# First MLP layer of the last two token groups by a seven-product scheme, with the former score banks as working space

## The chip, the cores and the metric

The kernel runs on one core of a Trainium2 chip. The core has a matrix engine (TensorE, here PE), a vector engine (VectorE, DVE), an engine for functions (ScalarE, ACT), GpSimd (POOL) and a queue engine (SyncE, SP). Matmul results land in PSUM, eight banks of 128 partitions x 512 f32; everything else lies in SBUF. The metric is the device time of one execution in microseconds, as the median of several runs.

## The reference

Attention with causal mask and 16 extra "beacon" keys, then a two-layer MLP with a sigmoid gelu on all 4608 tokens:

```
scores = (1/8) * q @ concat(beacon_k, k).T      # 8 batches, 8 heads, 576 queries, 592 keys, 64 wide
a      = softmax(masked scores)
x      = (a @ concat(beacon_v, v))  -> (4608, 512)
h      = x @ w_in                               # 512 -> 2048
g      = h * sigmoid(1.702 * h)
out    = g @ w_out                              # 2048 -> 512, float32
```

## The kernel before, in words

**Attention.** A set is four heads of one batch; there are 16 sets. `e_qk` (L437) writes a chunk of scores of a set into the tile `s`, which is four PSUM banks as one tile of 128 x 4 x 512 (L438); `e_exp` (L455) has ACT read all four banks and write the exponentials to SBUF (`E`, three buffers). POOL masks (L479), DVE adds up columns (L497), PE multiplies with the values (`e_av`, L528, matmul L534), DVE divides (L546 to L569) and writes the result, transposed, into `xT`, a ring of 2304 tokens.

**MLP.** Tokens go in groups, `GROUPS` (L576): two of 256 and then eight of 512; groups 8 and 9 are the last. The first layer of a group of 512 (`e_m1`, L582) has 16 tiles of 128 rows of `h`, each in a PSUM bank of its own and made of four matmuls of 512 columns (L593). ACT reads the bank and writes gelu to `g` (`e_gelu`, L611). The second layer of groups 2 to 9 is done already by a Strassen-Winograd scheme of seven products of halves (`products`, L947): DVE makes sums of quarters of `g` (`e_s`, L681, L658) and once of `w_out` (`e_t`, L665); `e_prod` (L693) does a product in four blocks of four matmuls of 256 columns (L707); `e_half` (ACT, L715) and `e_join` (DVE, L720) gather the products from PSUM, and `e_store4` (L728) has SP store a quarter of the group's output.

**PSUM.** Four banks are the score tile `s` (pool `pss`). The other four, `u0` to `u3` (pool `psu`), are a ring of `RING` = 4: every tile of `e_av`, `e_m1` and `e_prod` takes one of them (`ring_tile`, L349), which comes free when its last reader ("closer") is done.

**Order.** The kernel first describes all operations as `Op`s with engine, duration and dependencies. The order of each engine's queue is written out by hand in `ORDER` (L16), by numbers of operations. `Plan.run` (L147) goes through these lists with assumed durations; it settles which ring bank a tile takes and the order in which the instructions are emitted. The tile framework then puts in the semaphore waits, from what each instruction reads and writes of which tile, in the order of emission. The hardware runs every queue in its order, with these waits.

The lines that set bank and order:

```
def ring_tile(key):
    if key not in rings:
        i = plan.tiles[key]
        rings[key] = psu.tile([P, 512], F32, tag=f"u{i}", name=f"u{i}")
    return rings[key]
```

Of the kernel before, what the change touches and what calls it, by code (L numbers as in the profile page):

```python
# [10 lines left out]
ALU = mybir.AluOpType  # L11
# [7 lines left out]
        170, 173, 176, 145, 125, 148, 150, 177, 182, 188, 191, 227, 194, 197, 232, 183, 203, 234, 200, 178, 237,  # L19
        179, 206, 258, 241, 209, 184, 263, 185, 212, 265, 213, 248, 246, 268, 214, 215, 401, 251, 253, 272, 218,  # L20
        404, 275, 244, 279, 219, 220, 407, 282, 284, 277, 221, 414, 320, 296, 304, 290, 302, 292, 300, 298, 312,
        308, 294, 318, 314, 310, 306, 316, 426, 435, 423, 343, 338, 339, 340, 433, 431, 438, 344, 345, 359, 349,
        341, 464, 346, 350, 351, 352, 354, 574, 355, 429, 360, 361, 577, 356, 362, 357, 372, 365, 583, 474, 477,
        373, 366, 374, 367, 605, 480, 484, 375, 482, 607, 368, 506, 502, 488, 492, 610, 490, 486, 498, 504, 500,
        508, 514, 510, 516, 494, 496, 512, 534, 593, 596, 535, 536, 539, 540, 550, 541, 542, 537, 742, 545, 546,
        547, 548, 603, 745, 551, 552, 553, 599, 601, 619, 622, 748, 555, 556, 557, 558, 561, 755, 625, 627, 629,
        562, 563, 776, 568, 564, 569, 570, 571, 779, 764, 767, 659, 637, 641, 657, 649, 651, 647, 661, 635, 631,
        653, 805, 772, 770, 774, 643, 655, 633, 639, 645, 679, 680, 815, 818, 700, 681, 682, 684, 701, 915, 690,
        685, 686, 691, 692, 702, 918, 687, 693, 695, 703, 696, 924, 821, 823, 697, 698, 706, 946, 825, 707, 713,
        708, 709, 948, 934, 937, 714, 715, 716, 827, 951, 944, 940, 942, 853, 831, 833, 855, 857, 851, 843, 835,  # L30
        837, 847, 839, 845, 829, 849, 841, 1083, 960, 963, 875, 876, 880, 877, 878, 881, 882, 1086, 968, 966, 970,
        883, 1089, 902, 909, 903, 886, 891, 1096, 887, 888, 889, 892, 893, 1117, 904, 894, 905, 896, 897, 1120, 898,
        899, 910, 911, 1105, 1108, 1146, 912, 976, 994, 996, 972, 978, 1000, 992, 982, 974, 998, 990, 984, 988, 980,
        1002, 986, 1256, 1156, 1113, 1111, 1115, 1159, 1025, 1020, 1026, 1021, 1259, 1022, 1027, 1031, 1023, 1028,
        1265, 1164, 1162, 1166, 1041, 1042, 1287, 1036, 1047, 1032, 1048, 1033, 1037, 1038, 1034, 1039, 1289, 1054,
        1055, 1049, 1056, 1043, 1044, 1050, 1292, 1057, 1198, 1172, 1168, 1178, 1184, 1180, 1194, 1170, 1174, 1176,
        1275, 1278, 1182, 1186, 1196, 1188, 1190, 1281, 1301, 1285, 1283, 1304, 1216, 1217, 1221, 1192, 1222, 1227,
        1218, 1223, 1228, 1219, 1224, 1232, 1229, 1233, 1230, 1307, 1311, 1309, 1237, 1327, 1333, 1238, 1243, 1234,
        1244, 1235, 1323, 1239, 1245, 1250, 1251, 1341, 1240, 1246, 1252, 1253, 1337, 1405, 1315, 1331, 1343, 1411,
        1335, 1321, 1403, 1431, 1313, 1325, 1407, 1419, 1317, 1423, 1425, 1319, 1339, 1421, 1409, 1329, 1361, 1413,  # L40
        1366, 1382, 1429, 1362, 1363, 1401, 1367, 1364, 1427, 1368, 1383, 1372, 1369, 1373, 1374, 1375, 1388, 1377,
        1389, 1378, 1390, 1395, 1379, 1384, 1380, 1385, 1391, 1396, 1415, 1397, 1398, 1470, 1454, 1417, 1455, 1449,
        1471, 1450, 1451, 1476, 1452, 1456, 1477, 1457, 1478, 1460, 1461, 1462, 1463, 1465, 1466, 1467, 1468, 1472,
        1479, 1473, 1483, 1484, 1485, 1486,
# [3 lines left out]
        195, 198, 233, 235, 201, 204, 238, 180, 207, 259, 210, 264, 186, 266, 269, 216, 402, 405, 408, 222, 417,  # L48
        415, 297, 291, 303, 305, 301, 299, 293, 309, 321, 295, 319, 313, 315, 311, 307, 317, 436, 439, 342, 465,
        468, 575, 578, 584, 587, 606, 608, 503, 507, 489, 491, 493, 487, 499, 505, 509, 515, 517, 495, 501, 511,  # L50
        497, 513, 611, 538, 743, 746, 749, 756, 758, 777, 780, 660, 642, 638, 652, 658, 648, 650, 636, 632, 662,
        654, 806, 644, 634, 656, 640, 646, 809, 916, 683, 919, 928, 925, 947, 949, 952, 828, 832, 854, 856, 852,
        858, 834, 838, 844, 840, 836, 846, 830, 848, 850, 842, 1084, 879, 1087, 1090, 1099, 1097, 1118, 1121, 1147,
        1150, 977, 995, 979, 997, 993, 973, 975, 983, 991, 999, 989, 1001, 981, 1003, 985, 987, 1257, 1260, 1024,
        1269, 1266, 1288, 1290, 1293, 1199, 1179, 1173, 1181, 1185, 1195, 1171, 1169, 1175, 1177, 1183, 1187, 1197,
        1189, 1191, 1193, 1220, 1328, 1334, 1324, 1342, 1316, 1332, 1344, 1406, 1412, 1338, 1336, 1404, 1432, 1314,
        1408, 1420, 1318, 1424, 1326, 1426, 1320, 1340, 1422, 1410, 1330, 1322, 1414, 1430, 1402, 1365, 1428, 1416,
        1418, 1453,
# [3 lines left out]
        123, 163, 160, 124, 224, 169, 128, 166, 172, 175, 146, 147, 126, 149, 151, 225, 226, 398, 190, 193, 196,  # L62
        199, 255, 256, 257, 202, 205, 286, 242, 411, 287, 211, 208, 243, 399, 249, 247, 400, 250, 412, 254, 252,
        273, 245, 274, 280, 276, 413, 281, 285, 283, 278, 289, 461, 288, 462, 419, 580, 420, 463, 326, 327, 328,
        421, 322, 92, 323, 324, 422, 427, 428, 424, 425, 325, 330, 334, 329, 335, 432, 336, 331, 434, 337, 332, 333,
        470, 347, 582, 353, 471, 581, 472, 430, 473, 358, 363, 475, 476, 478, 479, 481, 485, 739, 483, 369, 376,
        370, 589, 752, 740, 590, 615, 518, 753, 921, 519, 754, 526, 591, 527, 520, 528, 592, 529, 521, 741, 522,
        597, 523, 594, 530, 595, 598, 531, 802, 532, 524, 533, 616, 543, 525, 604, 549, 617, 618, 554, 600, 620,
        602, 623, 624, 621, 559, 760, 628, 761, 762, 626, 630, 565, 763, 566, 768, 572, 765, 811, 812, 766, 803,
        804, 769, 773, 771, 671, 1080, 775, 672, 813, 922, 663, 814, 664, 675, 667, 816, 673, 819, 668, 669, 817,  # L70
        923, 665, 666, 820, 674, 676, 677, 1093, 670, 688, 694, 678, 930, 822, 824, 699, 931, 826, 932, 933, 704,
        710, 938, 939, 935, 936, 717, 711, 945, 941, 943, 1081, 956, 957, 958, 871, 1082, 1094, 1095, 959, 872, 873,
        867, 859, 961, 962, 964, 965, 860, 863, 1262, 1143, 861, 874, 862, 868, 864, 967, 865, 971, 866, 969, 884,
        869, 870, 1101, 1144, 890, 1145, 1102, 895, 1103, 1104, 900, 906, 1109, 907, 1110, 913, 1106, 1107, 1152,
        1153, 1004, 1154, 1005, 1155, 1264, 1006, 1263, 1016, 1012, 1017, 1157, 1114, 1112, 1013, 1018, 1116, 1160,
        1008, 1161, 1009, 1019, 1158, 1014, 1015, 1029, 1010, 1165, 1011, 1007, 1163, 1167, 1035, 1040, 1271, 1051,
        1045, 1058, 1052, 1297, 1272, 1273, 1274, 1298, 1299, 1276, 1279, 1300, 1200, 1204, 1280, 1201, 1277, 1205,
        1282, 1302, 1206, 1286, 1284, 1208, 1305, 1209, 1202, 1303, 1210, 1212, 1203, 1306, 1207, 1213, 1225, 1231,
        1308, 1312, 1214, 1310, 1215, 1211, 1236, 1247, 1241, 1248, 1254, 1349, 1345, 1350, 1346, 1347, 1353, 1351,
        1354, 1355, 1356, 1357, 1358, 1359, 1370, 1348, 1360, 1352, 1376, 1381, 1386, 1392, 1393, 1445, 1446, 1433,  # L80
        1399, 1437, 1434, 1438, 1447, 1435, 1441, 1442, 1436, 1443, 1444, 1439, 1448, 1440, 1458, 1464, 1469, 1480,
        1474, 1481, 1487,
    ],
    "POOL": [
        8, 10, 12, 14, 16, 17, 19, 21, 23, 25, 27, 29, 31, 33, 35, 37, 39, 41, 43, 45, 47, 110, 49, 51, 113, 114,
        53, 55, 57, 59, 133, 61, 136, 137, 63, 65, 67, 69, 71, 378, 230, 231, 229, 380, 382, 384, 386, 236, 388,
        390, 392, 239, 240, 394, 396, 261, 260, 262, 441, 443, 270, 267, 271, 449, 451, 453, 455, 457, 459, 403,
# [29 lines left out]
class Plan:  # L117
# [6 lines left out]
    def __init__(self, ring):  # L124
        self.ops = []
        self.ring = ring
        self.tiles = {}
        self.closers = {}
# [76 lines left out]
def kernel(  # L205
# [27 lines left out]
    HF = S // 2  # L233
    NKT = DMODEL // P
    NNT = DFF // P
    RING = 4

    NE, NB2, NB3 = 3, 2, 3

# [893 lines left out]
```

## Time and profile before

| what | value |
|---|---|
| median of 3 runs | 329.16 us (329.14 to 329.3) |
| span of the profiled execution, first to last instruction | 327.2 us |
| median less span (the profile shows no other time of its own execution) | 1.96 us |
| instructions | 9966 |
| granted TensorE clock, mean of the span | 0.999 |
| last score chunk's exponentials | before 250 us |
| last matmul, last join, end | 323.4, 324.1, 327.2 us |

Times inside the run count from the span's start. A line such as `L707 PE MATMUL u<-w,g ... x160 | 21.7, 273 | 0.0` is a group of instructions: source line, engine, operation, tiles written and read, shape, count; then busy us and mean ns of one; then the idle time of the engine in front of them and who ended it. PE's matmuls overlap in a pipeline, so a duration (273 ns) is longer than the step from one to the next. In the chain of waits every piece of time from the end of the run backwards is put down to the instruction that held up the next one.

### The profile page before, as it was taken

How to read it: one execution, taken by the hardware profiler on the slowest of the kernel's cores; microseconds unless marked ns; L12 is line 12 of the kernel's file. 1: busy time of each engine (PE TensorE's matmuls, PEld its weight loads, DVE VectorE, ACT ScalarE, POOL GpSimd, SP SyncE). 2: the span in 40 equal slices, each digit the busy share in tenths (PEclk: the TensorE clock that was granted, in tenths of full speed). 3: DMA queues.
4: the chain of work that ended last, by engine and by line, in shares of the span. 5: the costliest groups of instructions: out<-in, count | busy, mean ns of one | idle time of the engine just before them, and what ended most of it. 6: DMA issues, size and time to landing. Idle time of an engine off the chain costs nothing.

```text
span 327.2 us, 9966 instructions
## 1 busy us (share of the span) xinstructions
PE 314.6 (96%) x4364; PEld 214.7 (66%) x4364; DVE 237.2 (72%) x480; ACT 202.1 (62%) x236; POOL 113.9 (35%) x178
## 2 busy tenths in 40 slices
PE   6589999999999999999999999999999999999995
PEld 6467665545775477746878878547764776447884
DVE  4838798777987989977998798858558853006674
ACT  1676697678767586679666786868577212674010
POOL 8765478190419312941177019400042000000000
PEclk9999999999999999999999999999999999999999
DMA  7999999293424911792039709500120012000122
GB/s 126 159 201 211 204 186 184 37 123 107 99 72 64 190 34 34 79 198 43 7 53 178 119 4 124 154 2 3 34 98 0 2 34 83 15 0 2 65 98 97
DMA packets 58220, 28.83 MB, mean 88 GB/s; under 512 B 41280, under 2 KB 53568, under 8 KB 58176
## 3 DMA queue, kind: packets, MB, share of 16 engines
q0 software_dynamic: 47552, 18.49, 47.9%
q1 hardware_dynamic: 10560, 9.69, 9.2%
q8 instruction: 34, 0.56, 0.7%
q14 instruction: 10, 0.08, 0.1%
q10 hardware_dynamic: 64, 0.01, 0.0%
HBM read 37.22 MB, written 9.44 MB: 143 GB/s over the span
## 4 chain that ended last, share of the span: by engine, by line
PE 83%; DMA 6%; DVE 4%; POOL 3%; ACT 2%; issue 1%; ACTq 0%; POOLq 0%
PE u L593 34%; PE u L707 30%; PE u L534 9%; PE s L447 7%; PE u L638 3%; DMA w<-in_moe_w_out_dram 3%; DMA w<-in_moe_w_in_dram 3%; ACT E L458 1%; DVE sA L658 1%; DVE g L626 1%; POOL vb L378 1%; POOL w L384 0%; DVE bkn L403 0%; ACT L614 0%; DVE kT L418 0%
## 5 line engine op out<-in xcount | busy, mean ns | idle before, releaser
L593 PE MATMUL u<-xT,w 128*128 128x512 f16 (+1 forms) x704 | 130.6, 341 | 0.6 <-ACT g L614 0.5
L458 ACT ACTIVATE E<-s 128x2048 f16<-128x2048 f32 (+5 forms) x66 | 98.9, 1515 | 44.9 <-PE s L447 44.4
L614 ACT ACTIVATE g<-u 128x512 f16<-128x512 f32 x128 | 70.5, 598 | 53.7 <-PE u L593 53.2
L593 PEld LDWEIGHTS <-w 128*128 128x128 f16 x704 | 67.6, 98 | 54.3 <-issue 1.9
L479 POOL TENSOR_SCALAR_AFFINE_SELECT E<-E 128x512 f16<-128x512 f16 (+3 forms) x78 | 49.3, 665 | 110.8 <-ACT E L458 79.1
L723 DVE SCALAR_TENSOR_TENSOR osb<-u,osb 128x512 f32<-128x512 f32 x56 | 37.3, 683 | 24.5 <-PE u L707 22.5
L707 PEld LDWEIGHTS <-g 128*128 128x128 f16 x512 | 48.3, 98 | 9.3 <-issue 0.2
L707 PE MATMUL u<-w,g 128*128 128x256 f16 x384 | 50.6, 273 | 0.0
L447 PE MATMUL s<-qT,kT 32*128 32x32 f16 (+20 forms) x1376 | 34.6, 228 | 5.7 <-ACT E L458 2.8
L447 PEld LDWEIGHTS <-kT 32*128 32x128 f16 x1376 | 25.2, 92 | 22.5 <-issue 14.4
L707 PEld LDWEIGHTS <-sA 128*128 128x128 f16 x384 | 36.3, 98 | 5.3 <-issue 0.3
L707 PE MATMUL u<-tB,sA 128*128 128x256 f16 x256 | 35.1, 273 | 0.1
L658 DVE TENSOR_TENSOR sA<-g 128x512 f16<-128x512 f16 x32 | 12.9, 416 | 26.2 <-ACT g L614 26.2
L569 DVE TENSOR_TENSOR xT<-u,rz 128x352 f16<-128x352 f32 (+2 forms) x52 | 25.5, 517 | 6.5 <-PE u L534 6.3
L378 POOL DMA_DIRECT2D vb<-in_v_dram x32 | 27.4, 876 | 2.4 <-DMA qn<-in_q_dram 1.6
L534 PE MATMUL u<-E,vb 128*32 128x352 f16 (+8 forms) x928 | 27.4, 262 | 0.0
L497 DVE TENSOR_TENSOR zs<-zs,E 128x1344 f16<-128x1344 f16 (+2 forms) x36 | 22.7, 633 | 5.3 <-POOL E L479 4.4
L534 PEld LDWEIGHTS <-vb 128*32 128x32 f16 (+1 forms) x928 | 19.9, 96 | 5.5 <-issue 1.7
L418 DVE STREAM_TRANSPOSE kT<-kn 128x576 f32<-128x576 f32 x16 | 20.1, 1257 | 2.1 <-DMA kn<-in_k_dram 1.4
L418 DVE STREAM_TRANSPOSE qT<-qn 128x576 f32<-128x576 f32 x16 | 19.9, 1241 | 0.3 <-DMA qn<-in_q_dram 0.3
L546 DVE STREAM_TRANSPOSE zt<-u 128x224 f32<-128x224 f32 (+2 forms) x32 | 15.0, 470 | 5.9 <-PE u L534 5.8
L497 DVE TENSOR_TENSOR zs<-E 128x1856 f16<-128x1856 f16 x12 | 15.8, 1320 | 3.3 <-POOL E L479 3.3
(48 smaller groups left out, 252.3 us busy)
## 6 DMA issues: line engine op xcount, KB each, us to landing
out_dram<-osb SPq DMA_DIRECT2D x36, 256.0 KB, 2.4
kn<-in_k_dram POOLq DMA_DIRECT2D x16, 288.0 KB, 6.9
qn<-in_q_dram POOLq DMA_DIRECT2D x16, 288.0 KB, 6.5
vb<-in_v_dram POOLq DMA_DIRECT2D x24, 128.0 KB, 6.4
w<-in_moe_w_in_dram POOLq DMA_DIRECT2D x8, 256.0 KB, 9.4
w<-in_moe_w_out_dram POOLq DMA_DIRECT2D x4, 512.0 KB, 13.5
vb<-in_v_dram POOLq DMA_DIRECT2D x8, 112.0 KB, 5.0
vb<-in_v_dram POOLq DMA_DIRECT2D x8, 80.0 KB, 7.9
```

The lines of the kernel that those rows point to most:

```text
L378: nc.gpsimd.dma_start(out=t[0 : hi - lo, j, h0:h1, :], in_=v[b, h0:h1, lo:hi, :].rearrange("h n d -> n h d"),)
L418: nc.vector.transpose(out=f32(dst.rearrange("p n e -> p (n e)")).rearrange("p (r t) -> p t r", t=TR), in_=f32(src[:, :]).rearrange("p (t c ...
L447: nc.tensor.matmul(sc[:, h, o : o + w], kT[s % NB2][r : r + 32, j * P : (j + 1) * P, d], qT[s % NB2][r : r + 32, a : a + w, d], start=(d = ...
L458: nc.scalar.activation(out=Es[s][:, :, c0:c1], in_=ss[i][:, :, o : o + c1 - c0], func=AFT.Exp, scale=0.125,)
L479: nc.gpsimd.affine_select(out=blk, in_=blk, compare_op=ALU.is_ge, fill=0.0, base=off + (Nb if j == 0 else 0), pattern=[[0, Q], [1, w]], ch ...
L497: nc.vector.tensor_tensor(out=t, in0=E[:, :, Z0:S] if i == 1 else t, in1=E[:, :, wcol[i] : wcol[i] + S - a], op=ALU.add,)
L534: nc.tensor.matmul(u[32 * h : 32 * h + 32, a:e], lhs, src[0:kw, h, col : col + e - a], start=first, stop=last,)
L569: nc.vector.tensor_tensor(out=xT[:, 2 * hs + x : 2 * hs + x + n, t0 : t0 + w], in0=rings[("av", s, x, half)][:, 0 : n * w].rearrange("p (n ...
L593: nc.tensor.matmul(u[:, o + a - t0 : o + e - t0], w1t[:, kp, nt * P : (nt + 1) * P], xT[:, kp, a % XR : (e - 1) % XR + 1], start=(kp == 0) ...
L614: nc.scalar.activation(out=gts[g][:, n0:n1, 0:w], in_=rings[("m1", g, n0)][:, 0 : n * w].rearrange("p (n w) -> p n w", n=n), func=AFT.Gelu ...
L707: nc.tensor.matmul(u[:, HM * mt : HM * (mt + 1)], lhs[:, n, mt * P : (mt + 1) * P], rhs[:, n, :], start=(n == 0 and mt == 0), stop=(n == H ...
L723: nc.vector.scalar_tensor_tensor(out=osbs[(g, dst)][:, :], in0=rings[("p", g, p)][:, :], scalar=scale_of(g), in1=osbs[(g, src)][:, :], op0 ...
```

## The change

The first layer of groups 8 and 9 is done by the seven-product scheme too (`FAST = (8, 9)`), over halves of the 512 inputs, of the 2048 rows and of the 512 tokens. DVE makes four sums of quarters of `w_in` once (`e_ws`; three lie in an old `E` buffer, one in `bkf`) and four sums of quarters of the tokens per group (`e_xs`). For each of four row pairs `i`, a product (`e_part`) is four matmuls of 256 columns into a bank. Products that several results share are passed on: ACT copies the bank of product 1 into a second bank (`e_seed`), on which further products accumulate, and that one after product 6 into a third. Product 7 is copied to SBUF by ACT (`e_keep7`) and added by DVE to two banks, with the sums in SBUF (`e_sum7`, into the old `qn`/`kn` buffers, `hold`). Four gelus of ACT per row pair (`e_gelu4`) read two results from PSUM and two from SBUF.

Once the last score chunk's exponentials are done (`plan.late`), the four banks of `s` join the ring (`MORE = 4`) as slices of one last `s` tile. The lists of `ORDER` are the same up to 226 us of the plan and new behind that: second layer of group 6, the last score chunks, group 7 and all that follows. Other edits give operations clearer names or turn a gate into a list of gates.

```diff
-    RING = 4
+    RING, MORE = 4, 4
...
+    spare = []
     def ring_tile(key):
         if key not in rings:
             i = plan.tiles[key]
-            rings[key] = psu.tile([P, 512], F32, tag=f"u{i}", name=f"u{i}")
+            if i < RING:
+                rings[key] = psu.tile([P, 512], F32, tag=f"u{i}", name=f"u{i}")
+            else:
+                if not spare:
+                    spare.append(pss.tile([P, Q, 512], F32, tag="s", name="s"))
+                rings[key] = spare[0][:, i - RING, :]
         return rings[key]
...
+        for n in range(2):
+            for x in range(2):
+                nc.tensor.matmul(
+                    u[:, HM * n : HM * (n + 1)],
+                    lhs[:, x, (2 * i + n) * P : (2 * i + n + 1) * P],
+                    rhs[:, x, :],
+                    start=fresh and n == 0 and x == 0,
+                    stop=n == 1 and x == 1,
+                    skip_group_check=not fresh,
+                )
...
+    def e_seed(src, dst):
+        nc.scalar.mul(out=ring_tile(dst)[:, :], in_=rings[src][:, :], mul=1.0)
+    hold = [f32(t[:, 0 : 2 * 512]) for t in qn + kn]
+    def e_keep7(src, slot):
+        nc.scalar.mul(out=hold[slot], in_=rings[src][:, :], mul=1.0)
+    def e_sum7(src, slot, dst):
+        nc.vector.tensor_tensor(out=hold[dst], in0=rings[src][:, :], in1=hold[slot], op=ALU.add)
...
+            p1 = part(1, "a", [], True)
+            c1 = grab("seedb", 490, [p1], lambda: e_seed(key["a"], key["b"]), ring=key["b"])
+            p2 = part(2, "a", [c1])
+            gelu(0, 0, p2, key["a"], key["a"])
+            p6 = part(6, "b", [c1])
+            c2 = grab("seede", 490, [p6], lambda: e_seed(key["b"], key["e"]), ring=key["e"])
+            p7 = part(7, "f", [], True)
+            x7 = grab("keep7.", 480, [p7] + last, lambda: e_keep7(key["f"], slots[0]), closes=key["f"])
+            p5 = part(5, "e", [c2])
+            p4 = part(4, "b", [c2])
+            a1 = grab("sum22.", 605, [p5, x7] + last, lambda: e_sum7(key["e"], slots[0], slots[1]), "DVE")
+            g22 = gelu(1, 1, a1, slots[1])
+            p3 = part(3, "e", [a1])
+            gelu(0, 1, p3, key["e"], key["e"])
+            a2 = grab("sum21.", 605, [p4, x7] + last, lambda: e_sum7(key["b"], slots[0], slots[2]), "DVE", closes=key["b"])
+            g21 = gelu(1, 0, a2, slots[2])
...
+        if g in FAST:
+            fast(g, xs, old)
+            products(g)
+            return
...
+    plan.late = [x for n in range(len(CHUNKS[-1])) for x in [exps[(len(CHUNKS) - 1, n)]]]
```

## The prediction, as it was put on record

> **What bounds the kernel now.** I read the page first, its busy times:
>
> ```profile
> PE 314.6 (96%) x4364; PEld 214.7 (66%) x4364; DVE 237.2 (72%) x480; ACT 202.1 (62%) x236; POOL 113.9 (35%) x178
> ```
>
> TensorE (PE) works 96% of the 327.2 us span, and nobody else comes near. A mean hides stages, so next the busy time by stretches (columns: stretch, its length, then each engine's busy us, the granted clock, the DMA share and GB/s):
>
> ```profile
> 0.00:20.00 20.00, 12.86 (x289) 11.35 (x290) 12.23 (x33) 8.45 (x8) 15.59 (x29) 1.00 1.24 152
> ...
> 280.00:290.00 10.00, 10.00 (x48) 4.55 (x47) 0.00 (x0) 6.64 (x13) 0.00 (x0) 1.00 0.00 0
> 290.00:300.00 10.00, 10.00 (x62) 5.88 (x61) 4.81 (x13) 6.01 (x11) 0.00 (x0) 1.00 0.00 0
> ...
> 310.00:320.00 10.00, 10.00 (x90) 8.56 (x89) 7.47 (x19) 1.25 (x3) 0.00 (x0) 1.00 0.27 96
> ```
>
> Where the change works, from 227 us on, PE has no free time at all, while ScalarE (ACT) and VectorE (DVE) have room. The chain that ended last (start, us, what) says the same and gives the rates:
>
> ```profile
> 274.75 18.99 PE u L593 x88
> 293.75 0.44 PE u L707 x4
> ...
> 300.26 8.30 PE u L707 x76
> 308.55 0.86 PE u L593 x4
> ...
> 312.03 11.37 PE u L707 x104
> 323.39 0.02 issue
> 323.42 0.69 DVE osb L723
> ```
>
> It is PE without a break up to the last join and its store. 88 matmuls of 512 columns take 18.99 us, 0.2158 each; 104 of 256 columns take 11.37 us, 0.1093 each. So a microsecond of PE work removed here is one gained, and a microsecond in which PE waits here is one lost. The groups by line from 230 us on give what a reader of a bank costs (after the bar: busy us, mean ns of one):
>
> ```profile
> L593 PE MATMUL u<-xT,w 128*128 128x512 f16 x192 | 43.7, 379 | 0.0
> L614 ACT ACTIVATE g<-u 128x512 f16<-128x512 f32 x48 | 27.4, 598 | 37.9 <-PE u L593 37.8
> L707 PE MATMUL u<-w,g 128*128 128x256 f16 x160 | 21.7, 273 | 0.0
> L723 DVE SCALAR_TENSOR_TENSOR osb<-u,osb 128x512 f32<-128x512 f32 x27 | 17.9, 688 | 22.0 <-PE u L707 20.9 <-ACT osb L718 0.5 <-issue 0.3
> ```
>
> **What the change removes and adds on PE.** Groups 8 and 9 now take 2 x 64 matmuls of 512 columns in their first layer: 128 x 0.2158 = 27.62 us. Afterwards each takes 7 products x 4 row pairs x 4 matmuls of 256 columns, 224 in all: 224 x 0.1093 = 24.48 us. PE is relieved of 3.14 us; the second layer's work is unchanged.
>
> **ACT.** 32 gelus become 32 of the same 128x512 size (8 tiles x 4) plus 16 seeds and 8 copies of product 7: 24 x 0.598 = 14.4 us more. ACT has 10 - 6.64 and 10 - 6.01 us free in the two stretches above and more behind them, so as a mean this is covered by PE's work. Without that cover it would cost up to 14.4.
>
> **DVE.** 16 sums at about 0.69 (the join row, same operands), 8 token sums at 0.42 (128x512, the rows of L658) and 4 weight sums at 1.21 (L658's 128x2048) are 19.2 us more, spread over 240 to 316 us. DVE is idle in the whole of 280 to 290. Covered likewise.
>
> **Moved orders.** From 227 us on the blocks of groups 6 and 7, ten masks and the last score chunks are reordered too. No instruction is added by that, PE is saturated before and after it, and the last four PE blocks, the last join and the last store stay as they are. Nothing for these. POOL's and SP's DMAs are the same in number; SP's stores wait only for joins.
>
> **The price that the diff hides.** The four former score banks are handed out as slices of one tile `s` (`spare[0][:, i - RING, :]`), where the old ring banks are four tiles of their own. I went through the waits that the built program of the changed kernel carries. On the `u` banks each wait names the reader of the same bank. On `s` it does not: a matmul that opens or continues work in one of the four banks waits for the last ACT or DVE access to any of the four, and a reader waits for PE's last write to any of them. 86 PE blocks (42 tiles: 16 of the new scheme, 11 first-layer tiles of group 7, 11 second-layer products, 4 of attention) lie there, and 38 of them wait for an access to another bank. A second-layer product is hit in several of its four blocks: product 3 of group 7 waits at each one.
>
> What one such wait costs when PE arrives straight behind the block that the reader needs: the matmul's own drain, 273 - 109 = 0.164 us; from its end to the reader's start 0.037 (the last rows of the chain: 323.39 to 323.42); the read, 0.598 on ACT or 0.69 on DVE; and from the read's end to PE. The last is seen in the order of time where PE once waits for a gelu:
>
> ```profile
> 68.87 1.08 ACT L614 ACTIVATE g<-u 128x512 f16<-128x512 f32 x2
> ...
> 69.52 1.02 PE L593 MATMUL u<-xT,w 128*128 128x512 f16 x4 [0.49 <-ACT g L614]
> ```
>
> The first gelu ends at 68.87 + 0.60 = 69.47, PE starts at 69.52: 0.05. Together 0.85 us on ACT, 0.94 on DVE. A block of four 256-column matmuls put between hides 0.44 of it, two hide 0.87. Where the reader itself stands behind another instruction of its engine, or behind a tied access of its own, it is later by what that leaves. I followed the four queues of the changed program block by block with these numbers, beginning where the orders part. The 38 waits come out so:
>
> - 8 with nothing between, reader ACT: 0.85 to 0.91 each, 6.95 us (copy of product 7, then product 3 of group 7; gelus of group 7, then its next tiles)
> - 2 with nothing between, reader DVE: 0.98 each, 1.95 us
> - 10 with one block between: 0.42 to 0.51, 4.61 us
> - 3 whose reader stands behind a full read: 1.07 to 1.19, 3.36 us (the sum behind a join; a seed behind a gelu)
> - 5 whose reader is late by part of one: 0.63 to 0.75, 3.47 us
> - 4 likewise behind a block: 0.28 to 0.34, 1.22 us
> - 6 hidden but for 0 to 0.10: 0.38 us
>
> That is 21.9 us of PE standing still between 241 and 338 us of the changed run. The waits are the program's, so no faster engine avoids them. [...]
>
> **Sum.** Against the profiled execution: 327.2 - 3.1 + 21.9 = 346.0 us. The median of the runs, 329.16, lies 1.96 above that span (start and end of the run, unchanged). **348.0 us.**
>
> **Unknown sizes.** The price of a wait is good to some 0.05 us: 38 x 0.05 = 1.9 either way. No row shows ACT writing into a PSUM bank. Bounds: 0.49 (five gelus back to back take 2.56 us: (2.56 - 0.60)/4), and 0.69, the slowest 128x512 read here; I take 0.598, the nearest row (same engine, same size, PSUM source). About 10 waits end with a seed or behind one: -1.1 to +0.9. A sum of an f32 bank and an f32 SBUF tile I take as the join, 0.69; from the norm's row for 128x448 (0.62) it could not be under 0.62: -0.5. Own range: 344.5 to 351.
>
> **Rivals.**
>
> *The ties cost nothing and the scheme pays.* If PE mostly came so late to an `s` bank that the other banks had long been read, 327.2 - 3.1 + 1.96 = 326.0; following the same queues with waits on the same bank alone leaves about 1 us of stalls, 327.0. It is one mechanism: it decides from where PE's distance between dependent blocks passes 0.85 us, two blocks; the order has 0 or 1 block between at 20 of the 38. For it: ACT and DVE have room. Against it: PE runs three to five blocks in the time in which ACT does a tile's seed, copy and gelus, so it always catches up. 5 in 100 (4 faster, 1 within 0.2%).
>
> *The clock falls.* PE would idle some 17 to 22% of the stage in pieces of up to 1.2 us. If the granted clock were halved for a tenth of it, 9 us of matmul work would take 18: 357. Against it: in the first 20 us PE is busy 12.86 of 20 and the granted clock in that row is 1.00. [...] 4 in 100.
>
> *The seeds are slow.* If an ACT copy from bank to bank took double, 1.2 us, the 10 waits behind seeds grow by 0.6 each: 354. No row speaks for it. 6 in 100.
>
> **How the numbers follow.** Forecast 85 in 100, with a few of these outside its own range; the range 344 to 352 leaves out some 2 in 10 with the rivals. A measurement of this kernel can tell about 0.2% (0.7 us) from no change. Faster 0.04 and same 0.01 from the first rival, slower 0.95 from the rest.
>
> **What would show it.** After: PE's busy share in the stretches from 240 us on falls to about 83%, and PE's waits list lines writing `s` (the new product line, the second-layer line) released by ACT and DVE, some 17 us in about 32 places (the drain of 0.164 counts as busy), none over 1.3 us. The stalls sit on `s`, not on `u`. Matmuls of 256 columns still step by 0.109 and the clock row stays 1.00. If instead PE stays at 10.00 of 10 from 240 us on, the ties are not waited for and the forecast is wrong; if the waits are there but ACT's rows for the seed are long, it is the third rival.

## The result, and the profile after

| | time, median | to before, 95% interval | span of the profiled run |
|---|---|---|---|
| before | 329.16 us | | 327.2 us |
| after | 348.66 us | 1.0599, 1.0586 to 1.0613 | 346.5 us |
| forecast | 348.0 us (344 to 352) | | 346.0 us |

The change costs 19.5 us. Line numbers of the changed kernel are shifted: its first layer is L606, the second L720, the new products L809, the seed L819, the copy of product 7 L824, the sums L827, the new gelus L833, the joins L736; the gelus of group 7 are L627. Its busy times, from the page:

```profile
PE 318.8 (92%) x4460; PEld 225.6 (65%) x4460; DVE 255.6 (74%) x508; ACT 214.6 (62%) x260; POOL 113.9 (33%) x178
```

PE's busy time even grew by 4.2 us, although it does 3.1 us less work. Of this, 1.75 us lie in the first 20 us (14.61 against 12.86 us busy), where this execution's granted clock was 0.91 and that of before 1.00. The rest fits the drain of 0.164 us that counts as busy each time PE stops behind a block: some 35 such stops make 5.7 us. PE's share fell from 96% to 92%. By stretches (stretch, length, busy us of PE, weight loads, DVE, ACT and POOL, granted clock, DMA share, GB/s) the loss lies where it was expected:

```profile
230.00:240.00 10.00, 10.00 (x178) 7.65 (x170) 6.17 (x11) 6.41 (x5) 1.98 (x3) 1.00 0.09 29
240.00:250.00 10.00, 8.17 (x60) 4.36 (x58) 6.98 (x11) 4.74 (x7) 3.07 (x4) 1.00 0.07 26
...
280.00:290.00 10.00, 7.17 (x59) 5.70 (x59) 5.99 (x13) 5.07 (x10) 0.00 (x0) 1.00 0.16 54
...
310.00:320.00 10.00, 7.32 (x60) 5.68 (x59) 3.38 (x6) 5.78 (x10) 0.00 (x0) 1.00 0.00 1
```

Up to 240 us PE is as busy as before. From the moment at which the former score banks join the ring it is busy 7 to 9 tenths, and neither ACT nor DVE is full beside it: nobody is at work all the time, so the engines wait for each other. The chain that ended last shows how. Before, it was PE alone; now it changes engine at every step (start, us, what):

```profile
281.16 0.61 ACT kn L824
281.81 0.61 PE s L720 x4
282.51 0.70 DVE osb L736
283.26 0.61 PE s L720 x4
283.89 0.70 DVE osb L736
284.64 0.61 PE s L720 x4
285.27 0.61 ACT g L833
285.90 0.59 ACT s L819
286.53 0.60 PE s L720 x4
```

The four `PE s L720` rows are the four blocks of one product of group 7, all into one bank. Ahead of them and between them stand a copy of product 7 of group 8, two joins that read another product of group 7, a gelu and a seed of group 8. Nothing in the arithmetic ties these blocks to those reads and that write: the copy reads a second bank of the tile `s` and the seed writes it, both joins read a third, the gelu reads the fourth. PE's list of waits from 226 us on (line that waits, line waited for, us, times, longest) names only lines that write `s`; its first five rows:

```profile
PE s L809 <- DVE osb L736: 2.4, 3, 1.0
PE s L720 <- ACT s L819: 2.4, 4, 0.9
PE s L606 <- ACT g L627: 1.7, 3, 0.7
PE s L720 <- DVE osb L736: 1.5, 3, 0.8
PE s L720 <- ACT g L833: 1.2, 2, 0.7
```

All its 16 rows together are 15.7 us in 29 places, none over 1.0; none is for a `u` bank.

### The profile page after: what moved, and what is told of

Read it like the earlier page. It is cut to its first block, busy times and chain, and to the rows that moved or that the text cites. A ratio compares the mean times of both kernels' runs of the same rounds, so it can differ in the third digit from the quotient of the medians.

```text
span 346.5 us, 10246 instructions
## 1 busy us (share of the span) xinstructions
PE 318.8 (92%) x4460; PEld 225.6 (65%) x4460; DVE 255.6 (74%) x508; ACT 214.6 (62%) x260; POOL 113.9 (33%) x178
## 4 chain that ended last, share of the span: by engine, by line
PE 73%; DVE 10%; ACT 10%; issue 2%; DMA 2%; SPq 1%; DVEq 0%; ACTq 0%
PE u L606 22%; PE u L720 19%; PE s L460 8%; PE u L547 8%; PE s L720 5%; PE s L809 4%; PE u L651 3%; ACT E L471 3%; DVE osb L736 3%; PE s L606 2%; ACT g L833 2%; ACT g L627 2%; DMA bkf<-in_beacon_k_dram 1%; ACT s L819 1%; DVE sA L671 1%
## 5 line engine op out<-in xcount | busy, mean ns | idle before, releaser
L606 PE MATMUL u<-xT,w 128*128 128x512 f16 (+1 forms) x532 | 92.0, 328 | 0.6 <-ACT g L627 0.5
L606 PEld LDWEIGHTS <-w 128*128 128x128 f16 x576 | 55.1, 98 | 43.5 <-issue 5.0
L627 ACT ACTIVATE g<-u 128x512 f16<-128x512 f32 x85 | 45.9, 598 | 18.6 <-PE u L606 18.5
L720 PEld LDWEIGHTS <-g 128*128 128x128 f16 x512 | 48.4, 98 | 10.8 <-issue 3.9
L720 PE MATMUL u<-w,g 128*128 128x256 f16 x336 | 44.4, 273 | 0.0
L720 PEld LDWEIGHTS <-sA 128*128 128x128 f16 x384 | 36.3, 98 | 12.1 <-issue 6.5
L736 DVE SCALAR_TENSOR_TENSOR osb<-u,osb 128x512 f32<-128x512 f32 x45 | 30.1, 681 | 7.1 <-PE u L720 5.9
L582 DVE TENSOR_TENSOR xT<-u,rz 128x352 f16<-128x352 f32 (+2 forms) x50 | 24.7, 517 | 8.0 <-PE u L547 7.8
L720 PE MATMUL u<-tB,sA 128*128 128x256 f16 x208 | 28.7, 273 | 0.1
L547 PE MATMUL u<-E,vb 80*32 80x80 f16 (+8 forms) x888 | 26.7, 264 | 0.0
L559 DVE STREAM_TRANSPOSE zt<-u 128x224 f32<-128x224 f32 (+2 forms) x30 | 14.1, 472 | 5.3 <-PE u L547 5.1
```

The costliest lines, as they stand in the source:

```text
L547: nc.tensor.matmul(u[32 * h : 32 * h + 32, a:e], lhs, src[0:kw, h, col : col + e - a], start=first, stop=last,)
L582: nc.vector.tensor_tensor(out=xT[:, 2 * hs + x : 2 * hs + x + n, t0 : t0 + w], in0=rings[("av", s, x, half)][:, 0 : n * w].rearrange("p (n ...
L606: nc.tensor.matmul(u[:, o + a - t0 : o + e - t0], w1t[:, kp, nt * P : (nt + 1) * P], xT[:, kp, a % XR : (e - 1) % XR + 1], start=(kp == 0) ...
L627: nc.scalar.activation(out=gts[g][:, n0:n1, 0:w], in_=rings[("m1", g, n0)][:, 0 : n * w].rearrange("p (n w) -> p n w", n=n), func=AFT.Gelu ...
L720: nc.tensor.matmul(u[:, HM * mt : HM * (mt + 1)], lhs[:, n, mt * P : (mt + 1) * P], rhs[:, n, :], start=(n == 0 and mt == 0), stop=(n == H ...
L736: nc.vector.scalar_tensor_tensor(out=osbs[(g, dst)][:, :], in0=rings[("p", g, p)][:, :], scalar=scale_of(g), in1=osbs[(g, src)][:, :], op0 ...
```

## The experiments

The theory: the four banks are slices of one tile, the program's waits follow the tile, and so PE waits for reads of banks that it doesn't touch. The main rival: the new scheme's own chain (seed, copy, sum, gelu) is what PE waits for. A second rival: the clock.

**Four tiles instead of slices.** The pool of `s` is closed when the last scores are read, and a pool with four tiles of one bank is opened in its place; order and work are those of the changed kernel.

```diff
-    pss = ctx.enter_context(tc.tile_pool(name="pss", bufs=1, space=bass.MemoryType.PSUM))
...
+    psg = tc.tile_pool(name="pss", bufs=1, space=bass.MemoryType.PSUM)
+    pss = psg.__enter__()
...
-                    spare.append(pss.tile([P, Q, 512], F32, tag="s", name="s"))
-                rings[key] = spare[0][:, i - RING, :]
+                    psg.__exit__(None, None, None)
+                    spare.append(ctx.enter_context(tc.tile_pool(name="psr", bufs=1, space=bass.MemoryType.PSUM)))
+                rings[key] = spare[0].tile([P, 512], F32, tag=f"r{i}", name=f"r{i}")
```

> The changed kernel, with the four former score banks handed out as four tiles of one bank each instead of slices of one tile; same order, same work. Theory of the ties (a matmul into one bank waits for reads of the other three): the stalls on these banks go, PE is saturated again, and what is left is the removed PE work of 3.14 us: following the queues, 326.2 us, between 325.7 and 327. Rival, that the new scheme's own chain (seed, copy, sum, gelu on ACT and DVE) makes the stalls: waits on the same bank remain, and the time stays near 345 to 349. Rival, that the clock falls: it is 1.00 in the stretches of the changed kernel, so nothing to gain there.

Measured: 325.99 us, 0.9901 of before (0.9886 to 0.9916), 22.7 us faster than the changed kernel and as the theory had it. One stretch of its profile says why:

```profile
240.00:320.00 80.00, 80.00 (x784) 65.00 (x782) 59.48 (x122) 43.26 (x77) 3.07 (x4) 1.00 0.12 41
```

PE has no free time in it, and its list of waits from 226 us on is empty. All seeds, copies, sums and gelus are still there, in the same order, so the scheme's own chain costs PE nothing. The main rival falls. This is also the version that beats both kernels.

**Two tiles of two banks: half a dose.** The edit against the split kernel:

```diff
-                rings[key] = spare[0].tile([P, 512], F32, tag=f"r{i}", name=f"r{i}")
+                    spare.extend(spare[0].tile([P, 2, 512], F32, tag=f"r{j}", name=f"r{j}") for j in range(2))
+                rings[key] = spare[1 + (i - RING) // 2][:, (i - RING) % 2, :]
```

> As the split kernel, but the four banks are two tiles of two banks each: a half dose of the ties. Theory of the ties: a wait remains where the last access was to the other bank of the pair; following the queues, 7.0 us of stalls and 333.6 us (332.5 to 334.8). Rival of the scheme's own chain: no difference from the split or from the changed kernel. A rival that any slicing of a tile of several banks costs a fixed amount would give the changed kernel's 348.7.

Measured: 333.71 us, 1.0129 (1.0114 to 1.0144), where 333.6 was expected: 7.7 us over the split kernel, a third of what the four-bank tile costs. Its stretch and the first waits of its list (its lines are shifted by 3 against the changed kernel: L822 is the seed, L827 the copy of product 7):

```profile
240.00:330.00 90.00, 83.38 (x786) 65.11 (x784) 60.88 (x123) 43.91 (x77) 3.07 (x4) 1.00 0.12 43
```

```profile
PE r L609 <- ACT g L630: 1.3, 3, 0.7
PE r L723 <- ACT r L822: 0.7, 2, 0.4
PE r L812 <- ACT qn L827: 0.5, 1, 0.5
```

Fewer of the same waits, no longer than before: the loss goes with the number of accesses to a neighbour bank, not with slicing as such.

**The ties without the scheme, and their control.** The kernel before, with its plain first layer; the PSUM tiles of groups 8 and 9 are moved from the ring to the former score banks, once as slices of one tile, once as four tiles (made as in the split kernel).

```diff
...
-            rings[key] = psu.tile([P, 512], F32, tag=f"u{i}", name=f"u{i}")
+            if key[0] in ("m1", "p") and key[1] >= 8:
+                if not spare:
+                    spare.append(pss.tile([P, Q, 512], F32, tag="s", name="s"))
+                rings[key] = spare[0][:, i, :]
+            else:
+                rings[key] = psu.tile([P, 512], F32, tag=f"u{i}", name=f"u{i}")
```

> The kernel before, without the seven-product first layer; its PSUM tiles of groups 8 and 9 lie in slices of one four-bank tile (the former score banks) instead of four tiles of the ring. Same order, same work. Theory of the ties: the ties alone cost time; following the queues, 10.1 us of stalls between 258 and 334 us, 339.3 us (337.5 to 341). Rival that the scheme's own chain is the cause: 329.2, as before.

> The kernel before, without the seven-product first layer; its PSUM tiles of groups 8 and 9 lie in the four former score banks, but as four tiles of one bank each. The control to the run in which they were slices of one tile (367.3 us). Theory of the ties: same banks without the ties, so 329.2 us, as before (328.5 to 329.9). Rival, that the former score banks themselves, or moving there, cost time: toward 367 us.

Measured: slices 367.27 us, 1.1167 (1.1109 to 1.1225); four tiles 329.06 us, 1.0001 (0.9991 to 1.0010). With four tiles PE's list of waits from 250 us on is empty. So the banks are as good as the others, and the ties alone, with nothing of the new scheme, cost 38 us. The direction was as the theory has it, the size was not: I had expected 339.3. In that walk I had left ACT's and DVE's reads at their old times and let only PE move; where all three move, the same prices give 366, an estimate worked out after the run. The chain shows the pattern that the walk had missed (first layer L599, its gelu L620):

```profile
289.34 1.04 PE s L599 x4
290.38 0.02 issue
290.40 0.61 ACT g L620
291.01 0.04 issue
291.05 1.04 PE s L599 x4
```

Most first-layer tiles of 0.86 us from 279 to 310 us now stand alone in line with their gelu: one in 1.71 us (289.34 to 291.05), of which 0.85 is PE standing still. With all four banks in one tile and nothing else to do for PE, the ring is there little more than a ring of one; only here and there do two tiles run back to back.

**Seeds twice, in the split and in the tied kernel.** Each seed is copied two times in a row.

```diff
-        nc.scalar.mul(out=ring_tile(dst)[:, :], in_=rings[src][:, :], mul=1.0)
+        for _ in range(2):
+            nc.scalar.mul(out=ring_tile(dst)[:, :], in_=rings[src][:, :], mul=1.0)
```

> The split kernel, with each of the 16 seeds copied twice in a row by ACT (16 x about 0.6 us more on ACT, the result the same). Prediction's step: ACT's added work is covered, the seeds cost nothing. If ACT has room and the seeds lie off PE's path: within 0.5 us of the split kernel. If each seed is on the path only while PE has no other block ready: following the queues, 5.1 us of stalls and 331.2 us. If every seed is on PE's path: 16 x 0.5 to 0.6, 8 to 9.6 us, 334 to 336.

> The changed kernel as it is (four banks as slices of one tile), with each of the 16 seeds copied twice in a row by ACT. In the split kernel the same doubling cost 4.6 us. Theory of the ties: reads and copies now stand on PE's path also where no result of them is needed, so the doubling costs more here; following the queues, 7.3 us over the changed kernel, 355.9 us (354.5 to 357.5). Rival, that the stalls of the changed kernel hide ACT's additions (PE is waiting anyway): 4.6 us or less, below 353.3 us. Rival, that every seed is on the path: 16 x 0.6, 358.3 us.

Measured: split 330.62 us, 1.0045 (1.0028 to 1.0062), 4.6 us over the split kernel; tied 356.1 us, 1.0831 (1.0804 to 1.0859), 7.4 us over the changed one. The split kernel's waits from 226 us on, empty with single seeds, now hold the seeds and nothing else (L811 the new products, L822 the seed):

```profile
PE u L811 <- ACT u L822: 1.9, 5, 0.5
PE r L811 <- ACT r L822: 0.7, 2, 0.4
PE u L811 <- ACT r L822: 0.2, 1, 0.2
```

So ACT's added work is covered exactly as it stands and has little room: of 16 x 0.59 us of extra copies, half comes through. That is near the second of the three expected cases (331.2), not the first: the seeds cost nothing only as long as they are single. In the tied kernel the doubled seeds reach PE also through blocks that don't use them (first rows of its list from 226 us on; L820 is the seed):

```profile
PE s L720 <- ACT s L820: 5.5, 5, 1.5
PE s L809 <- DVE osb L736: 3.7, 3, 1.6
PE s L809 <- ACT s L820: 2.2, 2, 1.5
```

L720 is the second layer, which reads no seed; its waits for the seed's line went from 2.4 to 5.5 us. The 7.4 us are what the theory gave (7.3); the rival, that PE's waiting hides ACT's additions, gave 4.6 or less.

## Why the prediction was right, by its steps

- **Removed PE work, 3.14 us.** Right: where the ties are gone the time falls by 3.25 us, and the last matmul ends at 320.32 instead of 323.39, 3.07 earlier.
- **ACT and DVE covered.** Right as the orders stand (80.00 of 80 in the split kernel), but "free in the mean" was a weak reason: doubling 16 copies of 0.59 already cost 4.6 us.
- **The ties and their price.** Right, and shown by splitting them off: 22.7 us between the changed and the split kernel. From the starts of PE's matmuls, the stalls at blocks on `s` add up to some 22 us (21.9 forecast), and not because errors cancel: the eight with nothing between and an ACT reader are 6.9 us (6.95 forecast), the ten behind one block 4.6 (4.61). With nothing between, a stall is 0.85 us on ACT where nothing else delays the reader, as worked out, and 1.00 to 1.01 on DVE for the two that were put at 0.98; a block between leaves 0.41 to 0.54.
- **What PE's list would show.** Forecast 17 us in 32 places and PE at 83% from 240 us on; it shows 15.7 in 29, and PE 83.75 of the 100 us from 240 to 340. The list falls short of the stalls because the drain counts as busy.
- **The unknown operations.** A seed takes 0.58 to 0.61 us (0.598 taken), a sum 0.68 to 0.69 (0.69 taken). The rival of slow seeds had no ground.
- **The end of the run: the step that failed, by 0.6 us.** I costed the new order of the last joins at nothing. The chain's end reads:

```profile
336.87 1.63 issue
338.50 0.70 DVE osb L736
339.23 0.70 DVE osb L736
340.01 0.70 DVE osb L736
340.74 1.35 DVE osb L736 x3
```

  Seven joins run one behind the other, because the first of them starts only at 338.50. The 1.63 us ahead of it the profile calls issue, time in which it shows no wait, and the split kernel has the same (314.85 to 316.49), so why the joins start that late stays open. The last ends at 343.22, 1.32 behind PE's last block (341.90), where before it was 0.70 (323.39 to 324.11). The split kernel has the queue too, but ends 0.94 behind PE, so some 0.25 of it is the new order and the rest comes with the ties. This accounts for the span of 346.5 instead of 346.0. The median is a little further off, 0.66, because the profiled execution (348.27 us) was the fastest of the five.
- **The clock.** 1.00 in every stretch of the changed kernel's profile from 20 to 340 us, so the rival fell here; but see the last section. The argument against it was weaker than it seemed: it leaned on the granted clock of 1.00 in the first 20 us of before, and the same stretch of the changed kernel came to 0.91, with a clock of 0.50 from 13.93 to 17.34 us. That cost nothing in the end (at 222 us PE was 0.14 us ahead of before). The other four executions have mean clocks of 0.985 to 0.991 against 0.993, and spans of 346.8 to 348.0 us; no trace of them was kept.
- **Whose waits they were.** In the split kernel PE's list of waits from 226 us on is empty and the time is 325.99 us. With doubled seeds its trace has eight matmuls writing former score banks (`r`) without a wait from 274.83 to 275.87 us, while ACT reads such a bank from 275.08 to 275.68 and DVE from 275.62 on. The waits of the changed kernel were a matter of the program, not of the chip.

## What to carry to other kernels

Ask what object the waits are made for: banks handed out as slices of one tile are one resource, whatever the planner believes, and a false wait with no other block between cost 0.85 us behind a gelu and about 1.0 behind a join. Read the built program's waits for the tiles that a change introduces; they gave the 22 us of stalls which the arithmetic (3 us less work) and the busy shares could not give. And when a queue walk moves one engine, let all engines move: leaving two at their old times made one expectation here wrong by 28 us.

## What the runs showed of the hardware

In one stretch of each of two tied runs the mean granted clock was 0.83 and 0.84 (the first row is of the tied kernel with the plain first layer, the second of the one with doubled seeds). No wait of PE was over 1.4 us in the former from 255 us on, and none over 1.6 in the latter from 226 us on:

```profile
300.00:310.00 10.00, 6.32 (x20) 2.19 (x20) 0.00 (x0) 3.28 (x6) 0.00 (x0) 0.83 0.00 0
320.00:330.00 10.00, 7.28 (x52) 5.34 (x50) 4.29 (x7) 5.45 (x11) 0.00 (x0) 0.84 0.09 29
```

In the first stretch two blocks of four 512-column matmuls, at 302.65 and 304.97 us, took 1.64 and 1.68 us instead of 1.02, about 1.3 us more. PE's busy share over ten microseconds does not tell these stretches from others: from 280 to 290 us it was busy 5.62 of 10 in the former run and 6.54 in the latter, both at a clock of 1.00. What made the clock fall these runs do not show. The four executions of the former run took 365.9, 366.61, 367.93 and 370.53 us at mean clocks of 0.995, 0.990, 0.987 and 0.971, so a small part of its 38 us is the clock.

ACT copied a 128x512 f32 bank into another PSUM bank about as fast as into SBUF: medians of 0.582 to 0.590 us (the seeds of the changed kernel) against 0.592 to 0.598 (its copies of product 7).
